# Token-shift mixes on GpSimd, a two-step first relu tile and a new written order in a fused attention and channel-mix kernel

## The chip, the cores and the metric

The kernel runs on one core of a Trainium2 chip. The metric is the device time of one execution in microseconds (us), and the median of several runs is compared. A separate profiled execution leaves the trace; its span runs from its first to its last instruction.

The engines are named as the profile names them: PE (TensorE matmuls; PEld its weight loads), DVE (VectorE), ACT (ScalarE), POOL (GpSimd) and SP (SyncE, which issues DMAs here). Each works through its own instructions strictly in the order given; semaphores make it wait for others.

## The reference

Eight batches, eight heads, 576 positions, head width 64. First an attention with exponential features, then a channel mix with a token shift:

```python
def phi(x):
    proj = np.einsum('bhsd,df->bhsf', x, w_phi)
    proj = proj - np.max(np.abs(proj), axis=-1, keepdims=True)
    return np.concatenate([np.exp(proj), np.exp(-proj)], axis=-1)
q_p, k_p = (phi(q), phi(k))
kv = np.einsum('bhsf,bhsd->bhfd', k_p, v)
z = np.sum(k_p, axis=2)
num = np.einsum('bhsf,bhfd->bhsd', q_p, kv)
den = np.einsum('bhsf,bhf->bhs', q_p, z)[..., None] + 1e-06
...
# x: the attention output, heads side by side, [8, 576, 512]
xk = mu_k * x + (1.0 - mu_k) * x_prev      # x_prev: x shifted by one position
xr = mu_r * x + (1.0 - mu_r) * x_prev
k = np.maximum(xk @ w_k, 0.0)              # 512 -> 1024
v = k * k @ w_v                            # 1024 -> 512
r = 1.0 / (1.0 + np.exp(-(xr @ w_r)))
return (r * v).astype(np.float32)
```

## The kernel before

**Tiles and stages.** Attention works on pairs of heads: 8 batches of 4 pairs, n = 0 to 31. The channel mix works on whole batches (the relu layer, gate and value layer on 512 positions each) and, for every two batches, on one edge tile that takes the remaining 64 positions of both.

**How the order is made.** Every piece of work is an `op` with a name, and the string `ORDER` (lines 19 to 129) lists all names in the order in which they are issued. A word is `name/ENGINE:place+n@i`: the engine, where the op allows several; the PSUM slot it is put into; and n filler matmuls (on a tile of ones) issued ahead of it. `Plan.op` (line 139) keeps the function, the engines allowed and the slots. Dependencies, costs and port marks in an op's arguments were meant for whoever writes the order; the program doesn't read them (the waits come from what the instructions read and write). So each engine's order is exactly the written one.

**The names.** A number after a name is the head pair n; `b.i` is a batch and a part.

- `lk`, `lq`, `lv`: loads of k, q and v for a batch or part of it, issued by POOL (v by POOL or SP). `wk`, `wr`, `wv`: weights, by POOL.
- `pt`, `pa`, `pb`, `tr`: transposes of q and k, on PE with copies for the first two batches, as DMA transposes issued by SP later (line 355).
- `kp`, `qp` (PE, line 570): projections of k and q. `rk`, `rq` (DVE, lines 583 and 588): their maxima of absolute values. `ea`, `eb` (ACT, line 609): the two exponentials of k. `mh`, `mt`, `mc`: q's maxima as two bf16 parts, transposed and copied, so that `qt` (PE, lines 634 and 640) can project q again transposed with the maximum subtracted; `qa`, `qb` (ACT, line 647) its exponentials. `tp`, `rt`, `mhe`, `mte`, `mce`, `ekt`, `qte`, `eqe` do the same for the edge positions of a whole batch; `em`, `eme` are exponentials of k's maxima.
- `va`, `vb` (line 601, POOL or DVE): v times those, the two right-hand sides of `kv` (PE, line 660). `kc` copies kv. `nd` (PE, line 681) is the numerator and denominator, `ra`, `rd` (DVE, lines 689 and 693) the quotient `x_sc`.
- `xt`, `xe`, `xf` (pairs 0 to 7: PE transpose and copies) or `xz`, `xu` (later pairs: DMA transpose issued by SP and a copy) put x into `xs`, features on partitions, shifted by one position. `df` (line 730, POOL or DVE) is `diff` = x - x_prev. `xa`, `xb` (line 736, DVE) are the two mixes, diff times mu plus x_prev, into `xk` and `xr`: one instruction each, 64 in all.
- `h` (PE, line 815): relu layer of a batch, eight tiles of 128 features, four matmuls each. `rl` and `sq` (lines 206 to 214): relu and square into `kk`. `r`, `th`: gate and tanh. `v` (PE, line 848), `ob` (DVE), `so` (SP): value layer, product, store. `he`, `rle`, `sqe`, `re`, `the`, `ve`, `obe`, `soe`: the same for the edge tiles.

**PSUM.** There are three slots P of two banks each and two slots M of one bank. The attention's projections, kv and nd take P; h takes M; r and v take M, in the last two batches P.

**Buffers around the change.** `diff` has two buffers, `xs` two, `vt` (v as loaded) three, q and k as loaded (`nat`) and transposed (`qkT`) two each, `kk` two. The first k and q arrive in float32 in a `kk` buffer (line 362). Three float32 tiles that are used at the start only, `wph_f32`, `ident_f32` and `sel3` (lines 223 to 228), have places of their own.

Of the kernel before, what the change touches and what calls it, by code (L numbers as in the profile page):

```python
# [19 lines left out]
ident ones hk hq dve2 hk.d hq.d wphi wphi.d lk0.1 lk0.1.d lq0.1 lq0.1.d mus mus.d lk0.2 lk0.2.d dve3  # L20
lq0.2 lq0.2.d lv0.0/POOL lv0.0.d lk0.0.d/ACT lq0.0.d/DVE pt0.0:0+9@0 pt0.1:1 pa0/ACT pb0/DVE tr0
dve1 tp0.0:0+1@2 kp0:1 rt0.0 qp0:2 rk0 ekt0.0 mhe0.0/POOL lk1.0 lk1.0.d mte0.0:0+4@1 rq0 pt1.0:0 ea0
pt1.1:1 lq1.0 lq1.0.d pa1/ACT mce0.0/DVE pb1/DVE tr1 lv0.1/POOL lv0.1.d eb0 tp0.1:0+1@4 qp1:2
lv0.2/POOL lv0.2.d rt0.1 rq1 eme0.0 kp1:1+1@1 mh0/POOL ekt0.1 qte0.0:0 mhe0.1/POOL em0 rk1 eme0.1
eqe0.0 lk1.2 lk1.2.d mte0.1:2+3@1 pt2.0:1 mce0.1/ACT mt0:0 pt2.1:0 mh1/POOL pa2/DVE ea1 pb2/DVE tr2
va0/POOL pt3.0:1+1@4 mc0/DVE qp2:2 em1 pa3/DVE mt1:0 eb1 pt3.1:0 mc1/DVE vb0/POOL rq2 qt0:0 kp2:1
qa0 lq1.2 lq1.2.d pb3/DVE tr3 kv0:2 rk2 qb0 lk2.0 lk2.0.d pt4.0:0 mh2/POOL kc0/DVE ea2 pa4/DVE
va1/POOL mt2:0+2@1 qp3:2 mc2/DVE eb2 qt1:0 rq3 wk.0 wk.0.d qte0.1:0 pt4.1:1 eqe0.1 tp0.2:1 vb1/POOL
qa1 rt0.2 pt5.0:0 nd0:2 pb4/DVE tr4 ekt0.2 mhe0.2/POOL pa5/DVE pt5.1:1 ra0 qb1 rd0 lv1.0/POOL
lv1.0.d kp3:1 rk3 wk.1 wk.1.d wk.d eme0.2 kv1:2+1@0 em2 qp4:0 wr.0 wr.0.d kc1/ACT rq4 pb5/ACT tr5  # L30
mte0.2:2+1@0 xt0:0 wr.1 wr.1.d wr.d ea3 pt6.0:1 vb2/POOL mce0.2/DVE pa6/DVE qp5:0 eb3 qt2:2 rq5
qte0.2:1 mh3/POOL qa2 kp4:1 va2/POOL xe0/DVE mt3:0 xf0/DVE em3 mc3/DVE rk4 pt6.1:0 qb2 mh4/POOL
kv2:0 df0/POOL eqe0.2 kc2/DVE nd1:2 pb6/DVE tr6 ea4 nd2:0 lq2.0 lq2.0.d ra1 rd1 pt7.0:0 eb4 va3/POOL
pt7.1:1 ra2 pa7/DVE qt3:2 pb7/ACT tr7 rd2 mt4:1 xt1:0 vb3/POOL qa3 xf1/DVE xe1/DVE tp1.0:0 mc4/DVE
qb3 rt1.0 wv.0 wv.0.d kv3:1 kc3/ACT kp5:2 xa0 ekt1.0 xt2:0 nd3:1 rk5 mhe1.0/POOL xf2/ACT eme1.0
xe2/ACT df1/POOL ra3 ea5 rd3 xb1 eb5 xt3:0+7@1 mte1.0:1 qt4:0 xa1 xf3/ACT xe3/ACT qp6:2 xb0
mce1.0/ACT qa4 qt5:1+1@1 df2/DVE tr2.0 tr2.0.d tr8 tr9 qte1.0:0 df3/DVE qb4 xa2 em4 xa3 qp7:0+3@1
qa5 vb4/POOL rq6 h0.0:1+1@1 qb5 lv1.2/SP lv1.2.d va4/POOL rq7 tr2.2 tr2.2.d tr10 tr11 kp6:2
rl0.0/ACT kp7:1 eqe1.0 vb5/POOL rk6 kv4:0 sq0.0/ACT h0.1:1 kc4/ACT mh6/POOL rk7 ea6 va5/POOL nd4:0
eb6 h0.2:0 ra4 lk3.0 lk3.0.d rd4 rl0.1/ACT kv5:2 lv2.0/SP lv2.0.d xb3 rl0.2/ACT mt6:0 h0.3:1 kc5/ACT  # L40
xb2 mc6/ACT em6 ea7 sq0.1/DVE qp8:0 vb6/POOL nd5:2 rq8 eb7 r0.0:0 va6/POOL ra5 rl0.3/ACT rd5 tp2.0:1
th0.0 qt6:0 sq0.2/POOL rt2.0 qp9:2 qa6 h0.4:0 lq3.0 lq3.0.d rq9 qb6 r0.1:1 sq0.3/POOL ekt2.0
rl0.4/DVE qp10:0 qt7:2 wv.1 wv.1.d wv.d rq10 th0.1 kp8:1 vb7/POOL qa7 h0.5:0 rk8 mhe2.0/POOL qb7
kv6:0 rl0.5/DVE xt4:1 sq0.4/POOL kc6/ACT kp9:2 ea8 nd6:0 rk9 va7/POOL h0.6:0 eb8 tr3.0 tr3.0.d tr12
# [116 lines left out]
def kernel(  # L161
# [120 lines left out]
    st = {}  # L282
# [516 lines left out]
    def add_moe(b):  # L799
# [240 lines left out]
```

## Time and profile before

| | us |
|---|---|
| three runs | 278.89, 276.7, 277.08 |
| median | 277.08 |
| the profiled execution, its own time | 277.05 |
| its span | 275.3 |
| granted TensorE clock, mean | 1.00 of full |

The chain of work that ended last, by engine and by line, is this:

```profile
PE 76%; ACT 9%; DVE 7%; issue 2%; DMA 2%; SPq 1%; POOL 1%; DVEq 0%; ACTq 0%; POOLq 0%
PE ps_v L848 19%; PE ps_h L815 17%; PE ps_r L834 10%; PE ps_nd L681 6%; PE ps_kv L660 5%; ACT q L647 4%; PE ps_qT L634 2%; PE ps_he L903 2%; PE ps_k L570 2%; ACT k L609 2%; PE ps_qT L640 2%; PE ps_q L570 2%; DMA vt<-in_v_dram 2%; PE ps_ve L935 2%; DVE nmk L583 2%
```

How the views are to be read: part 1 of the page has each engine's busy time (a union of its records), part 2 cuts the span into 40 equal slices and gives the busy share of each in tenths. A group of instructions has its line, engine, operation, what it writes and reads, shapes and count, then busy time and mean duration in ns, then the engine's idle time just before them and what ended most of it. A wait has who waited for whom, the total in us, how often, and the longest. The records of an engine overlap a little[...]; so where instructions follow closely, the step from start to start tells the cost better than the duration.

### The profile page before, as it was taken

The numbers are of one execution on the slowest core, as the hardware profiler recorded it, in microseconds if no ns is written. First come the engines' busy times: TensorE is split into PE (matmuls) and PEld (weight loads), VectorE is DVE, ScalarE is ACT, GpSimd is POOL, SyncE is SP. The second block draws the span as 40 slices with busy tenths as digits, with TensorE's granted clock in tenths as the row PEclk, the third lists the DMA queues.
The fourth block names the chain that finished last, engine by engine and source line by source line (L and its number), as shares of the span: only waits on it lengthen the run. The fifth ranks groups of instructions, "written<-read, shape, count | busy, mean of one in ns | idle before, by whom it ended". The sixth has DMA issues, their size and how long they took to land.

```text
span 275.3 us, 8896 instructions
## 1 busy us (share of the span) xinstructions
PE 260.7 (95%) x3692; PEld 153.8 (56%) x3736; DVE 229.5 (83%) x366; ACT 223.2 (81%) x410; POOL 157.8 (57%) x218
## 2 busy tenths in 40 slices
PE   7798999999999999999999899999999999999994
PEld 2465745565755655665565466565556654444552
DVE  5899999999999999999999799888849799834222
ACT  3699999999999999989989899999997855552430
POOL 5899827995858766596648863844565205111010
PEclk9999999999999999999999999999999999999999
DMA  7999999999997897979998899775244523504044
GB/s 152 217 234 231 205 189 196 204 147 241 203 185 139 200 219 165 206 209 182 197 187 166 130 194 208 176 229 64 64 116 100 63 62 66 133 5 116 2 114 114
DMA packets 65880, 42.89 MB, mean 156 GB/s; under 512 B 47152, under 2 KB 57008, under 8 KB 65840
## 3 DMA queue, kind: packets, MB, share of 16 engines
q1 hardware_dynamic: 54544, 27.77, 48.8%
q0 software_dynamic: 10992, 14.12, 29.6%
q8 instruction: 29, 0.48, 0.7%
q10 hardware_dynamic: 304, 0.43, 0.5%
q14 instruction: 11, 0.09, 0.1%
HBM read 33.62 MB, written 9.44 MB: 156 GB/s over the span
## 4 chain that ended last, share of the span: by engine, by line
PE 76%; ACT 9%; DVE 7%; issue 2%; DMA 2%; SPq 1%; POOL 1%; DVEq 0%; ACTq 0%; POOLq 0%
PE ps_v L848 19%; PE ps_h L815 17%; PE ps_r L834 10%; PE ps_nd L681 6%; PE ps_kv L660 5%; ACT q L647 4%; PE ps_qT L634 2%; PE ps_he L903 2%; PE ps_k L570 2%; ACT k L609 2%; PE ps_qT L640 2%; PE ps_q L570 2%; DMA vt<-in_v_dram 2%; PE ps_ve L935 2%; DVE nmk L583 2%
## 5 line engine op out<-in xcount | busy, mean ns | idle before, releaser
L601 POOL TENSOR_TENSOR v<-vt,v 128x576 bf16<-128x576 f32 x62 | 73.5, 1205 | 36.2 <-ACT v L595 33.5
L609 ACT ACTIVATE k<-ps_k 128x1024 bf16<-128x1024 f32 x64 | 64.0, 1042 | 1.3 <-DVE nmk L583 1.1
L647 ACT ACTIVATE q<-ps_qT 128x1024 bf16<-128x1024 f32 x64 | 63.0, 1042 | 2.2 <-PE ps_qT L640 2.0
L815 PE MATMUL ps_h<-xk,wk_bf 128*128 128x512 bf16 x239 | 62.3, 380 | 1.1 <-issue 0.2
L848 PE MATMUL ps_v<-wv_bf,kk 128*128 128x512 bf16 x240 | 58.2, 379 | 0.8 <-issue 0.2
L730 POOL TENSOR_TENSOR diff<-xs 128x576 bf16<-128x576 bf16 x21 | 28.1, 1347 | 30.9 <-DVE xr L736 19.1
L588 DVE TENSOR_REDUCE nmq<-ps_q 128x8 f32<-128x1024 f32 x32 | 38.7, 1216 | 1.1 <-PE ps_q L570 1.0
L848 PEld LDWEIGHTS <-kk 128*128 128x128 bf16 x256 | 23.8, 98 | 27.1 <-issue 0.2
L583 DVE TENSOR_REDUCE nmk<-ps_k 128x8 f32<-128x1024 f32 x32 | 38.5, 1217 | 0.5 <-PE ps_k L570 0.2
L854 DVE SCALAR_TENSOR_TENSOR ob<-rt,ps_v 128x512 f32<-128x512 bf16 x32 | 21.7, 684 | 18.0 <-PE ps_v L848 12.9
L815 PEld LDWEIGHTS <-wk_bf 128*128 128x128 bf16 x256 | 22.7, 98 | 24.7 <-issue 0.5
L206 ACT ACTIVATE krelu<-ps_h 128x512 bf16<-128x512 f32 x40 | 23.8, 607 | 15.2 <-PE ps_h L815 15.2
L834 PE MATMUL ps_r<-wr_bf,xr 128*128 128x512 bf16 x121 | 31.9, 380 | 0.4
L840 ACT ACTIVATE rt<-ps_r 128x512 bf16<-128x512 f32 x32 | 19.4, 608 | 14.7 <-PE ps_r L834 12.2
L214 POOL TENSOR_TENSOR kk<-krelu 128x512 bf16<-128x512 bf16 x17 | 17.8, 1047 | 18.2 <-ACT krelu L206 13.8
L693 DVE TENSOR_TENSOR x_sc<-ps_nd,rden 128x640 bf16<-128x640 f32 x32 | 26.0, 818 | 0.7
L736 DVE SCALAR_TENSOR_TENSOR xk<-diff,mu_k_t,xs 128x576 bf16<-128x576 bf16 x32 | 26.3, 836 | 0.1
L736 DVE SCALAR_TENSOR_TENSOR xr<-diff,mu_r_t,xs 128x576 bf16<-128x576 bf16 x32 | 26.3, 837 | 0.0
L660 PE MATMUL ps_kv<-v,k 64*128 64x65 bf16 x1024 | 22.7, 190 | 1.6 <-DVE x_sc L693 0.7
L208 DVE TENSOR_SCALAR krelu<-ps_h 128x512 bf16<-128x512 f32 x24 | 16.4, 683 | 8.8 <-PE ps_h L815 8.0
L660 PEld LDWEIGHTS <-k 64*128 64x128 bf16 x1024 | 19.7, 94 | 6.7 <-DVE nmq L588 1.5
L212 ACT ACTIVATE kk<-krelu 128x512 bf16<-128x512 bf16 x35 | 22.1, 641 | 1.3 <-DVE krelu L208 1.2
(105 smaller groups left out, 416.9 us busy)
## 6 DMA issues: line engine op xcount, KB each, us to landing
out_dram<-ob SPq DMA_DIRECT2D x70, 128.0 KB, 2.5
vt<-in_v_dram SPq DMA_DIRECT2D x12, 576.0 KB, 4.7
nat<-in_k_dram POOLq DMA_DIRECT2D x6, 576.0 KB, 6.8
nat<-in_q_dram POOLq DMA_DIRECT2D x6, 576.0 KB, 7.9
vt<-in_v_dram POOLq DMA_DIRECT2D x3, 576.0 KB, 6.7
wk_bf<-in_moe_w_k_dram POOLq DMA_DIRECT2D x2, 512.0 KB, 8.7
wv_bf<-in_moe_w_v_dram POOLq DMA_DIRECT2D x2, 512.0 KB, 8.5
nat<-in_k_dram POOLq DMA_DIRECT2D x3, 288.0 KB, 6.3
```

What stands on the lines that cost most here:

```text
L583: nc.vector.tensor_reduce(t[:, j, :], s["k"].rearrange("p a (g f) -> p (a g) f", f=128), axis=AX.X, op=ALU.max, apply_absolute_value=True, ...
L588: nc.vector.tensor_reduce(t[:, j, :], s["q"].rearrange("p a (g f) -> p (a g) f", f=128), axis=AX.X, op=ALU.max, apply_absolute_value=True, ...
L601: (nc.vector if eng == "DVE" else nc.gpsimd).tensor_tensor(vb[:, a, pn, :, 0:64], vt[b, a // 2][:, a % 2, :].rearrange("p (s d) -> p s d", ...
L609: nc.scalar.activation(s[f"k{pn}"], s["k"].rearrange("p a (g f) -> p (a g) f", f=128), AF.Exp, scale=(1.0 if pn == 0 else -1.0))
L647: nc.scalar.activation(t.rearrange("f x (a p) -> f x a p", a=2), s["qT"].rearrange("f a (x p) -> f x a p", p=64), AF.Exp, scale=(1.0 if pn ...
L660: nc.tensor.matmul(ps[:, hh, pn * 65:(pn + 1) * 65], lhsT=s[f"k{pn}"][r, c, :], rhs=vb[r, a, pn, 2 * g + par, :], start=(pn == 0 and c == ...
L693: nc.vector.tensor_tensor(s["x"].rearrange("p (b s) d -> p b s d", b=2), s["ndv"][:, :, :, 0:64], s["rd"].to_broadcast([128, 2, 5, 64]), o ...
L730: (nc.vector if eng == "DVE" else nc.gpsimd).tensor_tensor(s["d"], xs[:, a, 64:64 + S], xs[:, a, 0:S], op=ALU.subtract)
L736: nc.vector.scalar_tensor_tensor(out=t[:, a, (b % 2) * S:(b % 2 + 1) * S], in0=s["d"], scalar=mu[:, a:a + 1], in1=xs[:, a, 0:S], op0=ALU.m ...
L815: nc.tensor.matmul(ps, lhsT=wk_bf[:, c, fc * 128:(fc + 1) * 128], rhs=xkt[bp][:, c, m0:m0 + 512], start=(c == 0), stop=(c == NDC - 1))
L834: nc.tensor.matmul(ps, lhsT=xrt[bp][:, c, m0 + ci * 128:m0 + (ci + 1) * 128], rhs=wr_bf[:, c, :], start=(c == 0), stop=(c == NDC - 1))
L848: nc.tensor.matmul(ps, lhsT=s["kk"][:, fc, ci * 128:(ci + 1) * 128], rhs=wv_bf[:, fc, :], start=(fc == 0), stop=(fc == NFC - 1))
```

## The change

**Mixes.** `xa` and `xb` may now be placed on POOL. There a mix is two instructions: a product of `diff` and mu into a float32 tile `emix` (one buffer), and the sum of that and `xs`. The new order places 13 of the `xa` and 12 of the `xb` on POOL; 39 mixes stay on DVE as they were.

**First relu tiles.** Tiles 0 and 1 of the first batch, formerly `h0.0` and `h0.1` in two M slots, become one pair in a P slot, summed in two ops: `ha0` takes three of the four input chunks for both tiles (6 matmuls, needs `xa0` to `xa2`), `hb0` the fourth (2 matmuls, needs `xa3`).

**Constants.** `wph_f32`, `ident_f32` and `sel3` move into the `kk` buffer that already takes the first k and q.

**Dependencies given to the order's writer.** `ea` may stand ahead of `rk`, and `ekt` ahead of `rt`.

**Order.** `ORDER` is written anew from end to end. How often an op kind is on which engine, where this differs:

| op | before | after |
|---|---|---|
| xa, xb | DVE 64 | DVE 39, POOL 25 |
| df | DVE 11, POOL 21 | DVE 24, POOL 8 |
| va, vb | DVE 2, POOL 62 | DVE 11, POOL 53 |
| sq | DVE 12, ACT 35, POOL 17 | DVE 23, ACT 28, POOL 13 |
| sqe | DVE 1, ACT 4, POOL 3 | DVE 1, ACT 5, POOL 2 |
| rl, rle | DVE 25, ACT 47 | DVE 27, ACT 45 |
| kc | DVE 15, ACT 17 | DVE 12, ACT 20 |
| mc, mce | DVE 12, ACT 16 | DVE 19, ACT 9 |
| mhe | POOL 10 | DVE 5, POOL 5 |
| xe | DVE 5, ACT 3 | DVE 7, ACT 1 |
| xu | DVE 2, ACT 9, POOL 13 | DVE 1, ACT 12, POOL 11 |
| pa, pb | DVE 12, ACT 4 | DVE 13, ACT 3 |
| lv (issues) | POOL 5, SP 12 | POOL 3, SP 14 |
| filler matmuls | 36 | 30 |

The order around the first relu tiles, before and after (other stretches are rewritten in the same way):

```diff
-mce1.0/ACT qa4 qt5:1+1@1 df2/DVE tr2.0 tr2.0.d tr8 tr9 qte1.0:0 df3/DVE qb4 xa2 em4 xa3 qp7:0+3@1
-qa5 vb4/POOL rq6 h0.0:1+1@1 qb5 lv1.2/SP lv1.2.d va4/POOL rq7 tr2.2 tr2.2.d tr10 tr11 kp6:2
...
+xe1/DVE mhe1.0/DVE xf1/ACT kc3/ACT kp5:0 df1/DVE xf2/ACT ekt1.0 nd3:2 rk5 xb1/POOL eme1.0
+mte1.0:1+1@1 tr2.0 tr2.0.d tr8 tr9 ra3 ea5 mce1.0/DVE xe2/DVE qte1.0:1+1@1 rd3 qp6:1 xa1/POOL eqe1.0
+rq6 qt4:2+1@0 eb5 xt3:0 lv1.0/SP lv1.0.d qp7:1 xb0/DVE em4 qt5:0 xf3/ACT lv1.2/SP lv1.2.d qa4
+xe3/DVE df2/DVE lv2.0/SP lv2.0.d df3/DVE qb4 tr2.2 tr2.2.d tr10 tr11 xa2/DVE qa5 xa3/DVE ha0:2+7@1
+xb2/DVE qb5 hb0 xb3/DVE h0.2:0 rl0.1/ACT rq7 va4/POOL rl0.0/ACT qp8:0 rl0.2/ACT qp9:2 rq8 kp6:1
```

The code:

```diff
-    wph_f32 = consts.tile([128, F], FP, name="wph_f32")
+    kk0 = mm.tile([128, NFC, 512], BF, name="kk").rearrange("p a x -> p (a x)").bitcast(FP)
+    X2 = 2 * (S // 64) * D
+    wph_f32 = kk0[:, X2:X2 + F]
...
-    ident_f32 = consts.tile([128, 128], FP, name="ident_f32")
+    ident_f32 = kk0[:, X2 + F:X2 + F + 128]
...
         def mix(i):
-            def f():
+            def f(eng):
                 dct, mu = ((xkt, mu_k_t), (xrt, mu_r_t))[i]
                 t = dct[bp]
+                if eng == "POOL":
+                    e = mid.tile([128, S], FP, name="emix", bufs=1)
+                    nc.gpsimd.tensor_scalar(e, s["d"], mu[:, a:a + 1], None, op0=ALU.mult)
+                    nc.gpsimd.tensor_tensor(t[:, a, (b % 2) * S:(b % 2 + 1) * S], e, xs[:, a, 0:S], op=ALU.add)
+                    return
                 nc.vector.scalar_tensor_tensor(out=t[:, a, (b % 2) * S:(b % 2 + 1) * S], in0=s["d"],
                                                scalar=mu[:, a:a + 1], in1=xs[:, a, 0:S],
                                                op0=ALU.mult, op1=ALU.add)
...
+        def h2(c0, c1):
+            def f():
+                if c0 == 0:
+                    s["h2"] = ptile(("P", "hh"), "ps_hh")
+                else:
+                    s["kk"] = mm.tile([128, NFC, 512], BF, name="kk")
+                    for fc in range(2):
+                        s[fc] = s["h2"][:, fc, :]
+                        s["kr", fc] = mm.tile([128, 512], BF, name="krelu", bufs=BUFS["krelu"])
+                for fc in range(2):
+                    for c in range(c0, c1):
+                        nc.tensor.matmul(s["h2"][:, fc, :], lhsT=wk_bf[:, c, fc * 128:(fc + 1) * 128],
+                                         rhs=xkt[bp][:, c, m0:m0 + 512], start=(c == 0), stop=(c == NDC - 1))
+            return f
...
+            if b == 0 and fc < 2:
+                mo, hn = ("P", "hh"), "hb0"
+                if fc == 0:
+                    op("ha0", "PE", 1.3, ("un",) + t, h2(0, 3), mixa[0:3] + ["wk.d"], chain="h", alloc=[("P", mo)])
+                    op("hb0", "PE", 0.44, ("un",) + t, h2(3, 4), mixa + ["wk.d"], chain="h",
+                       alloc=[("krelu", ("krelu", f"{b}.{i}")) for i in range(2)] + [("kk", ("kk", b))])
```

## The prediction

> **What bounds the kernel now.** I read the page's parts 1, 2 and 5 first, then busy time in six stretches, then VectorE's order of time, then the waits. Part 1 and the 40 slices of part 2:
>
> ```profile
> PE 260.7 (95%) x3692; PEld 153.8 (56%) x3736; DVE 229.5 (83%) x366; ACT 223.2 (81%) x410; POOL 157.8 (57%) x218
> PE   7798999999999999999999899999999999999994
> DVE  5899999999999999999999799888849799834222
> ACT  3699999999999999989989899999997855552430
> POOL 5899827995858766596648863844565205111010
> ```
>
> TensorE looks busy from start to end, but its records overlap. In the last 40 us, where only 512-column matmuls run, one starts every 0.216 us. At such start-to-start steps all its needed work is 237.4 us: relu layer h 55.3, value layer v 55.3, gate r 27.6, their edge tiles 17.6, kv 18.2, nd 20.8, k and q projections 14.7, second projection 14.1, rest 13.8. The span is 275.3, so 38 us are lost. About 3.8 stand at the end (last product, last store). Placing the nd matmuls in the trace against the work ordered ahead of them gives the rest: 22.4 lost by 42.6 us, 25.2 by 60, 30.2 at nd19 (140.9 us), 34.1 at nd31 (228.4 us).
>
> What holds TensorE up? Busy time by stretch (us, then PE, PEld, DVE, ACT, POOL):
>
> ```profile
> 60.00:100.00 40.00, 39.28 (x669) 24.68 (x678) 38.57 (x60) 38.29 (x66) 29.99 (x42) 1.00 1.02 189
> 100.00:150.00 50.00, 49.37 (x766) 29.39 (x771) 48.21 (x67) 45.82 (x88) 33.15 (x39) 1.00 0.98 196
> 150.00:200.00 50.00, 48.80 (x738) 28.90 (x745) 43.30 (x65) 46.85 (x83) 29.24 (x40) 1.00 0.71 147
> 200.00:232.00 32.00, 31.63 (x431) 18.59 (x433) 25.74 (x46) 23.73 (x43) 11.94 (x18) 1.00 0.39 78
> ```
>
> VectorE is 96% busy to 150 us, 87% in the next 50. GpSimd always has room. VectorE's own steps, from its order of time (start, us, operation, count):
>
> ```profile
> 37.95 0.82 DVE L730 TENSOR_TENSOR diff<-xs 128x576 bf16<-128x576 bf16 x2
> 38.69 1.54 DVE L736 SCALAR_TENSOR_TENSOR xk<-diff,mu_k_t,xs 128x576 bf16<-128x576 bf16 x2
> 40.15 2.35 DVE L588 TENSOR_REDUCE nmq<-ps_q 128x8 f32<-128x1024 f32 x2
> ```
>
> Start to start, a difference takes 0.37, a mix 0.73, and a maximum (its next group starts at 42.41) 1.13. Now D is the VectorE work ordered up to the last result that a TensorE step needs, and P the TensorE work ordered ahead of that step. TensorE's loss there is at least D - P plus VectorE's idle time so far. At h0.0, D - P is 17.1 and the idle time 4.2; at nd19 it is 19.9 and 10.2, together 30.1 against the 30.2 found. So **VectorE is the wall up to about 141 us**; after that TensorE has a nearly full queue, and loses 3.9 more up to nd31.
>
> **What the Trainium skill says.** "SBUF — State Buffer", section "Who interferes with whom": VectorE with two SBUF inputs and a GpSimd instruction that reads SBUF exclude each other for a whole instruction. The trace agrees: one xk mix took 1.77 us instead of 0.81 because GpSimd had started 0.01 us earlier (one xr took 1.83 at 232 us); the other 62 mixes met nothing.
>
> ```profile
> 150.65 1.77 DVE L736 SCALAR_TENSOR_TENSOR xk<-diff,mu_k_t,xs 128x576 bf16<-128x576 bf16 x1
> 150.64 1.17 POOL L601 TENSOR_TENSOR v<-vt,v 128x576 bf16<-128x576 f32 x1 [0.86 <-ACT v L595]
> ```
>
> "GPSIMD Engine Reference", "Elementwise — side-by-side cycle accounting": about 2.6 cycles an element at 1.2 GHz for two inputs (estimate for 576: 1.25 us), about 1.8 at best for a tight one-input loop (0.86). The rows agree with the first: 1.2 and 1.35; no row shows the second.
>
> ```profile
> L601 POOL TENSOR_TENSOR v<-vt,v 128x576 bf16<-128x576 f32 x62 | 73.5, 1205 | 36.2 <-ACT v L595 33.5
> L730 POOL TENSOR_TENSOR diff<-xs 128x576 bf16<-128x576 bf16 x21 | 28.1, 1347 | 30.9 <-DVE xr L736 19.1
> L736 DVE SCALAR_TENSOR_TENSOR xk<-diff,mu_k_t,xs 128x576 bf16<-128x576 bf16 x32 | 26.3, 836 | 0.1
> ```
>
> **The change, part by part.**
>
> *Mixes.* 25 mixes leave VectorE: 25 x 0.73 = 18.3 us. On GpSimd the sum is a v-like operation, 1.12 from start to start. The product has no row: from below 0.67, by the slope between a 4-element cast (0.187) and a 63-element copy (0.237); from above 1.23, the step of a difference. I take 0.8. The sum waits for the product on its own engine, 0.08 as in the cast and subtract of mhl. One mix is then 2.0 us (1.85 to 2.45), 25 are 50. The single float32 buffer costs nothing more, its only user being GpSimd's ordered queue.
>
> *What comes back.* 13 differences (13 x 0.37 = 4.8), 9 v products (9 x 0.61 = 5.5), 11 squares (11 x 0.33 = 3.7), and smaller copies and casts, less three kv copies, about 3.2. VectorE's sum falls by only 1, 220.9 to 220.0. ScalarE loses 6 squares on balance, 2 x copies and some small ones, and gains 3 kv and 3 shift copies: 210.8 to 205.5. GpSimd gains 50 and loses 13 x 1.23 + 9 x 1.12 + about 9: 154 to 169, of 275. So **the totals decide nothing; the order does**.
>
> *Order.* The same reckoning with the new order, D - P at its worst steps: ha0 16.6 (h0.0 had 17.1), qte2.0 18.7 (19.3), qt12 20.4 (r1.0 had 19.8), qt18 19.1, v2.0 18.3, kv20 18.2 (nd19 had 19.9), v3.0 17.9, v4.0 16.7. With the idle times seen at equal D: 20.9 (before 21.3), 25.3 (25.9), 27.7 (26.9), 28.9 against 30.1 near P = 100 to 110. VectorE stays the wall longer, to v4.0 (D 180.3, about 195 us). There its idle time, growing at the 0.56 us in 10 that it showed from 35 to 142 us, would be 13.2, and TensorE's loss 29.9; before, it was 33 there. With 1.0 more to nd31 (as before from 195 us) and 3.8 at the end: 237.4 + 29.9 + 1.0 + 3.8 = 272.1, or 3.2 under the span. I keep half, 1.7: for 50 us more every VectorE wait counts in full, and new waits on GpSimd join.
>
> *GpSimd's queue.* xa0, xb1 and xa1 stand on it just ahead of the first relu step. df1 ends near 33.7, two mixes end near 37.7, and VectorE's xa2 near 39.7: cover 2 us, gone if a mix takes 2.45 and its queue is also 1 us late. Behind them wait va4 and vb4, which kv4 needs, and the queue's k and q loads. xa7 and xb7 stand ahead of h1.0 and r1.0, xb31 ahead of r7.0 with about 0.5 us to spare.
>
> *First relu tiles.* ha0 starts after three k mixes instead of four, hb0 adds the fourth quarter: the same 8 matmuls, so 0 us of work, at most 0.7 earlier (one mix). It holds a two-bank slot until both relus have read it; the projections have two others.
>
> *The rest.* Two loads of v move from GpSimd's to SP's queue behind the first DMA transpose (3.4 us of issue); their landing took 4.7 and va4 starts near 42.5, so they are covered if that transpose starts by 34, as the earlier q load allows (it waited for that load until 36.7). The constants moved into a kk buffer cost nothing: its next user comes after 80 us. k's exponential ahead of its maximum concerns the first two pairs; the maximum then waits for ScalarE. Six fewer filler matmuls (30 against 36) save nothing, being run in idle time.
>
> Sum: 275.3 - 1.7 = 273.6 of span. The run profiled took 277.05, 1.75 over its span, as good as the median 277.08. So **275.3**.
>
> **Rivals.** *Bigger gain*: the whole 3.2 comes, and spacing removes the 2 us that the two blocked mixes lost: span 270.5 to 272, time 273 (272.2 to 273.8). For it: D - P. Against it: the second block lay in the tail, off the wall.
>
> *No change*: GpSimd takes the place. The waits
>
> ```profile
> POOL v L601 <- ACT v L595: 33.5, 12, 7.3
> POOL diff L730 <- DVE xr L736: 19.1, 3, 12.7
> ```
>
> are room that does not lie where the mixes want it: before 34 us GpSimd idled only 4 us. If its queue makes kv4 to kv9 1.7 us late, the gain is gone: 277 (276 to 278).
>
> *Slower*: the port. GpSimd's long SBUF instructions grow from 103 (about 115 us) to 126 (134), the VectorE instructions with two SBUF inputs from 90 to 98. One that comes at random finds GpSimd running about 0.58 of the time to 230 us, and waits half of one, 0.55: 0.32 each. Of about 73 on the wall, a quarter losing their place would cost 5.8 us. Against it: 2 of 90 blocked now, so the written order holds on the chip. For it: no trace shows the product, and 0.45 more of it would shift all that stands behind it. Three blocks eat the gain, eight more make it 1% slower: 281 (279.9 to 284).
>
> That the change isn't made is out: the instruction lists show 25 products and 25 sums on GpSimd.
>
> **Numbers.** Likeliest, small gain: 0.50, own range 273.3 to 277.3. Bigger gain 0.14, no change 0.14, slower 0.22. About 1%, 2.8 us, is what these runs (276.7 to 278.9) can tell from no change: faster is under 274.3, slower over 279.9. A third of the first case and all but a little of the second are faster: 0.30. Within 1%: 0.46. Slower: 0.24, the slower case and a rest. The range from 271.8 to 281.5 takes in the bounds of the product (25 x 0.45 = 11 us on GpSimd, mostly in its idle time) and most of the slower case.
>
> **What would show it.** Right: the first ps_h starts near 39.8 instead of 40.7; nd19 near 139; VectorE busy over 92% from 150 to 195 us; the product 0.7 to 0.95 us; few VectorE mixes, squares or v products over 1 us. Wrong: the product near 1.2; many such stretched instructions, or GpSimd's idle time before v gone and kv held by v; VectorE under 95% busy before 150 us because of DMA or GpSimd.

## The result and the profile after

The changed kernel takes **302.24 us** (median of 4 executions, 301.33 to 305.41), the kernel before on the same chip 277.41 us: a ratio of 1.0908, with a 95% interval of 1.0811 to 1.1005. It is slower. The forecast of 275.3 us missed by 27 us; its range ended at 281.5. The profiled execution took 301.34 us, with a span of 299.6 (before 275.3). Some executions of a kernel are disturbed and show a lower granted clock: here and below times, ratios and intervals are those of the undisturbed ones, the median of all executions stands in brackets where it differs, and a star marks a kernel whose trace is of a disturbed one. Ratios are of means, so they can differ a little from the quotient of the medians.

Parts 1 and 2 of the page of the changed kernel:

```profile
PE 266.1 (89%) x3679; PEld 154.5 (52%) x3726; DVE 246.0 (82%) x391; ACT 219.7 (73%) x401; POOL 199.5 (67%) x225
...
PE   7888867979998979987999899979988999989994
...
DVE  5999999999998899779998998788899894444512
...
POOL 8699894787799793999059639729964028946000
PEclk9999997999999999999999999979999999999998
```

VectorE's busy time was to fall by about 1 us and has grown from 229.5 to 246.0. GpSimd has 199.5 where the forecast's sum gave 169 (in steps). TensorE's granted clock dips in slices 7 and 27 (and in the last); before, no slice was below 9. Its mean is 0.985, 1.00 before. Over the 237.4 us of needed matmuls that would be 3.6 us (an estimate, which supposes that a matmul takes longer as the clock is lower; no run isolates it). The groups say which instructions grew, first the products in the page's part 5, then VectorE's mixes in the list of VectorE's groups (after the bar busy us and mean ns):

```profile
L743 POOL TENSOR_SCALAR emix<-diff,mu_k_t 128x576 f32<-128x576 bf16 x13 | 22.4, 1721 | 14.3 <-DMA out_dram<-ob 7.3
...
L743 POOL TENSOR_SCALAR emix<-diff,mu_r_t 128x576 f32<-128x576 bf16 x12 | 20.8, 1736 | 2.9 <-DVE diff L735 1.8
```

```profile
L746 DVE SCALAR_TENSOR_TENSOR xr<-diff,mu_r_t,xs 128x576 bf16<-128x576 bf16 x20 | 21.6, 1086 | 1.2 <-POOL diff L735 1.1
L746 DVE SCALAR_TENSOR_TENSOR xk<-diff,mu_k_t,xs 128x576 bf16<-128x576 bf16 x19 | 17.7, 947 | 2.0 <-POOL diff L735 2.0
```

Two things stand here. The product takes 1.72 us; the forecast took 0.8 and held 1.23 for the upper bound. And a mix on VectorE, 0.836 on the mean before, has a mean of 1.086 or 0.947. Its undisturbed duration is still 0.81: 10 of the 39 are longer than 1 us, up to 3.18. Over all VectorE instructions with two SBUF inputs (mixes, differences, value products, squares), the excess over the undisturbed durations of 0.81, 0.45, 0.75 and 0.42 us is 15.0 us in 19 instructions, against 2.0 in 2 before.

The chain of work that ended last has changed as well. It accounts for only a third of the span, so its shares are not to be compared one by one, but TensorE's 76% of before are 14%, and GpSimd's 1% are 11%, with the product first among GpSimd's lines:

```profile
PE 14%; POOL 11%; DVE 5%; issue 2%; ACT 1%; DVEq 0%; POOLq 0%; ACTq 0%
PE ps_v L873 5%; POOL emix L743 5%; PE ps_h L825 3%; PE ps_r L859 2%; POOL kk L217 2%; POOL xk L744 2%; DVE v L606 2%; POOL xr L744 1%; PE ps_he L936 1%; PE ps_nd L686 1%; DVE ob L879 1%; DVE kk L217 1%; PE ps_ve L968 1%; DVE xk L746 0%; DVE krelu L211 0%
```

Busy time by stretch (us, then PE, PEld, DVE, ACT, POOL, clock):

```profile
35.00:60.00 25.00, 19.91 (x277) 10.99 (x278) 24.69 (x30) 19.22 (x34) 18.21 (x18) 0.93 0.85 152
60.00:100.00 40.00, 36.43 (x649) 22.39 (x658) 37.98 (x63) 36.53 (x61) 33.11 (x42) 1.00 1.06 178
100.00:150.00 50.00, 44.06 (x703) 26.09 (x713) 44.96 (x67) 42.59 (x75) 36.23 (x40) 1.00 0.96 185
150.00:200.00 50.00, 45.90 (x698) 27.72 (x707) 45.90 (x70) 42.82 (x84) 33.27 (x35) 0.98 0.91 168
```

TensorE's busy time from 100 to 150 us was 49.37 and is 44.06. Up to 100 us VectorE is counted busy nearly all the time (24.69 of 25 us, 37.98 of 40), but stretched time counts as busy in that. From 100 us on no engine is full, which is what a chain that passes from engine to engine looks like.

The loss of TensorE, reckoned as in the prediction (time of a step less the work ordered ahead of it), in us; five of the kernels run later stand beside it:

| loss at | before | after | a_sum_only | a_sum_em4_lv | a_tt_product | a_dve_reduce | a_sum_em4_lv_reduce |
|---|---|---|---|---|---|---|---|
| kv4 | 22.4 | 27.7 | 26.1 | 21.5 | 27.1 | 24.4 | 20.9 |
| nd13 | 28.2 | 38.0 | 33.2 | 30.3 | 39.7 | 31.5 | 27.6 |
| nd21 | 31.7 | 45.2 | 37.9 | 35.3 | 44.2 | 36.7 | 31.1 |
| nd31 | 34.1 | 55.4 | 40.1 | 37.5 | 49.0 | 43.5 | 33.2 |

The loss is spread over the whole run. Its first step, 5.3 us up to kv4, can be read instruction by instruction. VectorE and then GpSimd of the changed kernel, in order of time (start, us, operation, count, idle time ahead):

```profile
37.49 1.21 DVE L746 SCALAR_TENSOR_TENSOR xr<-diff,mu_r_t,xs 128x576 bf16<-128x576 bf16 x1
38.62 0.45 DVE L205 COPY xs<-ps_x 128x576 bf16<-128x576 bf16 x1
39.11 1.91 DVE L735 TENSOR_TENSOR diff<-xs 128x576 bf16<-128x576 bf16 x2
40.94 3.35 DVE L746 SCALAR_TENSOR_TENSOR xk<-diff,mu_k_t,xs 128x576 bf16<-128x576 bf16 x2
44.22 3.91 DVE L746 SCALAR_TENSOR_TENSOR xr<-diff,mu_r_t,xs 128x576 bf16<-128x576 bf16 x2
```

```profile
37.35 1.72 POOL L743 TENSOR_SCALAR emix<-diff,mu_k_t 128x576 f32<-128x576 bf16 x1
39.16 1.54 POOL L744 TENSOR_TENSOR xk<-emix,xs 128x576 bf16<-128x576 f32 x1
40.81 2.88 POOL L606 TENSOR_TENSOR v<-vt,v 128x576 bf16<-128x576 f32 x2
43.63 0.82 POOL L329 DMA_DIRECT2D nat<-in_k_dram  x1
44.48 2.30 POOL L606 TENSOR_TENSOR v<-vt,v 128x576 bf16<-128x576 f32 x2
```

Two k mixes took 1.54 us before and take 3.35 here, two r mixes (at 46.01 us before) 1.53 and now 3.91, behind value products of GpSimd; the second difference, 1.54 instead of 0.45, is behind GpSimd's sum. TensorE waits for the third and the fourth k mix, 1.58 us inside `ha0` and 0.62 ahead of `hb0`. In the lines that follow, the third holds four matmuls that start 0.43 us apart in place of 0.22, and the last waits for VectorE's maximum, which stands behind the r mixes:

```profile
42.71 1.02 PE L840 MATMUL ps_hh<-xk,wk_bf 128*128 128x512 bf16 x4 [1.58 <-DVE xk L746]
44.35 0.64 PE L840 MATMUL ps_hh<-xk,wk_bf 128*128 128x512 bf16 x2 [0.62 <-DVE xk L746]
44.78 1.92 PE L825 MATMUL ps_h<-xk,wk_bf 128*128 128x512 bf16 x4
...
49.32 0.40 PE L575 MATMUL ps_k<-wph,qkT 64*128 64x128 bf16 x8 [1.66 <-DVE nmq L593]
```

The three waits and the slower matmuls add up to 4.7 us, against 5.3 for the step. The granted clock is lower in the stretch from 40 to 50 us (0.83; before it was 1.00):

```profile
40.00:50.00 10.00, 6.14 (x41) 2.56 (x39) 10.00 (x7) 5.36 (x9) 7.23 (x9) 0.83 1.10 154
```

Before the change GpSimd had no work while VectorE did its differences and five of the mixes (35.8 to 40.2 us). It sat waiting for ScalarE's exponentials `em4`:

```profile
34.02 1.27 POOL L730 TENSOR_TENSOR diff<-xs 128x576 bf16<-128x576 bf16 x1
40.19 3.42 POOL L601 TENSOR_TENSOR v<-vt,v 128x576 bf16<-128x576 f32 x3 [4.89 <-ACT v L595]
```

The new order has `em4` further ahead on ScalarE, so the value products are free earlier, and run into the mixes.

### The profile page after: what moved, and what is told of

The parts are those of the page before. It is cut to its first block, busy times and chain, and to the rows that moved or that the text cites. A ratio compares the mean times of both kernels' runs of the same rounds, so it can differ in the third digit from the quotient of the medians.

```text
span 299.6 us, 8907 instructions
## 1 busy us (share of the span) xinstructions
PE 266.1 (89%) x3679; PEld 154.5 (52%) x3726; DVE 246.0 (82%) x391; ACT 219.7 (73%) x401; POOL 199.5 (67%) x225
## 5 line engine op out<-in xcount | busy, mean ns | idle before, releaser
L606 POOL TENSOR_TENSOR v<-vt,v 128x576 bf16<-128x576 f32 x53 | 63.0, 1210 | 18.4 <-ACT v L600 15.4
L825 PE MATMUL ps_h<-xk,wk_bf 128*128 128x512 bf16 x230 | 60.4, 384 | 3.8 <-ACT krelu L209 1.4
L873 PEld LDWEIGHTS <-kk 128*128 128x128 bf16 x256 | 23.8, 98 | 27.1 <-issue 0.4
L865 ACT ACTIVATE rt<-ps_r 128x512 bf16<-128x512 f32 x32 | 19.1, 601 | 24.4 <-PE ps_r L859 24.4
L825 PEld LDWEIGHTS <-wk_bf 128*128 128x128 bf16 x248 | 22.2, 98 | 28.2 <-issue 5.1
L859 PE MATMUL ps_r<-wr_bf,xr 128*128 128x512 bf16 x118 | 33.8, 394 | 1.8 <-POOL xr L744 0.8
L743 POOL TENSOR_SCALAR emix<-diff,mu_k_t 128x576 f32<-128x576 bf16 x13 | 22.4, 1721 | 14.3 <-DMA out_dram<-ob 7.3
L209 ACT ACTIVATE krelu<-ps_h 128x512 bf16<-128x512 f32 x37 | 21.9, 603 | 12.7 <-PE ps_h L825 8.9
L698 DVE TENSOR_TENSOR x_sc<-ps_nd,rden 128x640 bf16<-128x640 f32 x32 | 26.1, 821 | 0.6
L665 PE MATMUL ps_kv<-v,k 64*128 64x65 bf16 x1024 | 21.8, 191 | 2.8 <-DVE v L606 0.9
L575 PEld LDWEIGHTS <-qkT 64*128 64x128 bf16 x512 | 17.5, 95 | 12.0 <-issue 9.0
L743 POOL TENSOR_SCALAR emix<-diff,mu_r_t 128x576 f32<-128x576 bf16 x12 | 20.8, 1736 | 2.9 <-DVE diff L735 1.8
L735 POOL TENSOR_TENSOR diff<-xs 128x576 bf16<-128x576 bf16 x8 | 10.8, 1351 | 17.7 <-DVE xk L746 11.6
L746 DVE SCALAR_TENSOR_TENSOR xr<-diff,mu_r_t,xs 128x576 bf16<-128x576 bf16 x20 | 21.6, 1086 | 1.2 <-POOL diff L735 1.1
## 6 DMA issues: line engine op xcount, KB each, us to landing
nat<-in_k_dram POOLq DMA_DIRECT2D x3, 288.0 KB, 7.9
nat<-in_q_dram POOLq DMA_DIRECT2D x3, 288.0 KB, 8.1
```

The source lines that it names most:

```text
L606: (nc.vector if eng == "DVE" else nc.gpsimd).tensor_tensor(vb[:, a, pn, :, 0:64], vt[b, a // 2][:, a % 2, :].rearrange("p (s d) -> p s d", ...
L665: nc.tensor.matmul(ps[:, hh, pn * 65:(pn + 1) * 65], lhsT=s[f"k{pn}"][r, c, :], rhs=vb[r, a, pn, 2 * g + par, :], start=(pn == 0 and c == ...
L698: nc.vector.tensor_tensor(s["x"].rearrange("p (b s) d -> p b s d", b=2), s["ndv"][:, :, :, 0:64], s["rd"].to_broadcast([128, 2, 5, 64]), o ...
L743: nc.gpsimd.tensor_scalar(e, s["d"], mu[:, a:a + 1], None, op0=ALU.mult)
L825: nc.tensor.matmul(ps, lhsT=wk_bf[:, c, fc * 128:(fc + 1) * 128], rhs=xkt[bp][:, c, m0:m0 + 512], start=(c == 0), stop=(c == NDC - 1))
L859: nc.tensor.matmul(ps, lhsT=xrt[bp][:, c, m0 + ci * 128:m0 + (ci + 1) * 128], rhs=wr_bf[:, c, :], start=(c == 0), stop=(c == NDC - 1))
```

## The experiments

Two causes were to be told apart: the **length** of the mix on GpSimd (its queue is late for what waits behind it), and the **port** that GpSimd and VectorE's two-input instructions exclude each other from. Behind them stand the places of single steps in the order. All times are medians; ratios compare with the kernel before on the same chip. The excess is read from one trace of each kernel.

| kernel | executions | us | ratio, 95% interval | excess in stretched VectorE instructions, us (number) |
|---|---|---|---|---|
| the changed kernel | 4 | 302.2 | 1.0908, 1.0811 to 1.1005 | 15.0 (19) |
| a_sum_only | 2 | 285.2 | 1.0267, 1.0142 to 1.0393 | 5.2 (6) |
| a_tt_product | 2 | 290.8 | 1.0470, 1.0279 to 1.0661 | 15.1 (17) |
| a_all_dve | 2 | 296.7 | 1.0682, 1.0608 to 1.0755 | 7.3 (8) |
| a_em4_late * | 3 of 4 | 300.3 (301.1) | 1.0806, 1.0717 to 1.0895 | 14.9 (18) |
| a_sum_em4 * | 3 of 4 | 282.5 (283.4) | 1.0160, 1.0070 to 1.0250 | 1.7 (3) |
| a_dve_reduce | 2 of 4 | 288.5 (290.7) | 1.0368, 1.0267 to 1.0469 | 6.1 (9) |
| b_pool25 | 4 | 312.8 | 1.1236, 1.1160 to 1.1313 | 13.0 (18) |
| a_sum_em4_lv | 4 | 281.2 | 1.0117, 1.0065 to 1.0169 | 2.5 (3) |
| a_act_em4_lv | 4 | 288.0 | 1.0360, 1.0301 to 1.0418 | 4.3 (8) |
| a_tt_em4_lv | 4 | 287.6 | 1.0363, 1.0319 to 1.0407 | 11.5 (16) |
| a_one_step | 4 | 304.5 | 1.0957, 1.0891 to 1.1023 | 15.4 (19) |
| a_sum_reduce | 9 of 20 | 278.9 (282.4) | 1.0021, 0.9993 to 1.0050 | 0.2 (1) |
| a_sum_em4_lv_reduce | 13 of 20 | 277.7 (278.8) | 0.9996, 0.9965 to 1.0026 | 0.7 (2) |

### What the product costs

`a_prices` does the product in four forms in turn; the third takes 0.5 in mu's place.

```diff
-nc.gpsimd.tensor_scalar(e, s["d"], mu[:, a:a + 1], None, op0=ALU.mult)
+kind 0: nc.gpsimd.tensor_scalar(e, ..., mu[:, a:a + 1], ...)   # float32, line 748
+kind 1: the same into a bfloat16 tile                          # line 751
+kind 2: nc.gpsimd.tensor_scalar(e, ..., 0.5, ...)              # line 753
+kind 3: nc.gpsimd.tensor_tensor(e, s["d"], mu[:, a:a + 1].to_broadcast([128, S]), op=ALU.mult)  # line 755
```

> The changed kernel with the 25 products in four forms in turn, to price them: float32 result with mu from memory (as it is, 1.72 us), bf16 result with mu from memory, float32 result with the constant 0.5 (leaves mu out of those mixes), and a two-input product with mu broadcast. If the float32 result costs the time, the bf16 form is under 1.2; if reading mu does, the constant form is under 1.2; if the one-input operation is slow as such, both stay near 1.7 and the two-input form near 1.25.

Its groups on GpSimd:

```profile
L753 POOL TENSOR_SCALAR emix<-diff 128x576 f32<-128x576 bf16 x6 | 9.9, 1650 | 1.0 <-ACT tk L507 0.8
L751 POOL TENSOR_SCALAR emix<-diff,mu_k_t 128x576 bf16<-128x576 bf16 x4 | 6.9, 1724 | 7.5 <-DVE diff L735 7.3
...
L748 POOL TENSOR_SCALAR emix<-diff,mu_r_t 128x576 f32<-128x576 bf16 x3 | 5.3, 1778 | 0.1
```

and the form with two inputs, with minimum, median and maximum in ns:

```profile
L755 POOL TENSOR_TENSOR emix<-diff,mu_r_t x4: 1137/1148/1148, 101.1 to 213.5; 128x576 f32<-128x576 bf16 x4
```

The kernel took 299.6 us in its one execution. The result's type makes no difference (1.724 against 1.72), the scalar from a tile 0.07 us. It is the one-input form itself that is slow here, as the third case of the expectation had it: with one input less it takes 1.72 us where the two-input product takes 1.15. "GPSIMD Engine Reference", section "Engine selection", of the Trainium skill says that one-input work is "roughly line-rate" on GpSimd, and the forecast, which put one input below two, agrees with that. For this form and size the measurement decides against it: 1.72 us is twice the 0.86 estimated for a one-input loop in the prediction.

### How much is the length

```diff
 a_sum_only
-nc.gpsimd.tensor_scalar(e, s["d"], mu[:, a:a + 1], None, op0=ALU.mult)
-nc.gpsimd.tensor_tensor(t[...], e, xs[:, a, 0:S], op=ALU.add)
+nc.gpsimd.tensor_tensor(t[...], s["d"], xs[:, a, 0:S], op=ALU.add)
 a_tt_product
-nc.gpsimd.tensor_scalar(e, s["d"], mu[:, a:a + 1], None, op0=ALU.mult)
+nc.gpsimd.tensor_tensor(e, s["d"], mu[:, a:a + 1].to_broadcast([128, S]), op=ALU.mult)
 a_all_dve
-xa0/POOL ... xb1/POOL ... xa1/POOL ...
+xa0/DVE ... xb1/DVE ... xa1/DVE ...
```

> The changed kernel with the product left out of the 25 mixes on GpSimd: each is the sum of diff and x_prev alone, one instruction (so those parts of xk and xr are not scaled by mu). Length theory (a mix on GpSimd takes 3.0 us instead of the 2.0 that the forecast used, and all the loss hangs on that): with 1.3 us in its place the time falls below the forecast's premise, to 273 to 279 us, and VectorE's stretched mixes nearly vanish. Order theory (the new order loses by its loads, slots and places whatever a mix costs): it stays above 292. Lock theory (the number of two-input meetings counts, not the length): about half of the loss stays, 285 to 291.

> The changed kernel with the product of the 25 mixes written as a two-input product of diff and mu broadcast along the row (same result). Length theory: if that product takes about 1.25 us like the other two-input forms, a mix is 2.5 us, and the time lies well between: 284 to 294 us. Order theory: no change beyond 2 us from 302. Lock theory: as many meetings, each as long as before for the sum and 0.5 shorter for the product: 296 to 301.

> The changed kernel with all 64 mixes on VectorE, every instruction at the same place in the order. VectorE gets 18.3 us of work back, about 14 of it ahead of v4.0, the last step where it was the wall. Length theory: no long GpSimd mixes, so the loss is only that extra work: 237.4 + 29.9 + 14 + 5 = 286 span, 284 to 291 us. Order theory: 302 plus most of the extra work, above 305. Lock theory: two-input instructions on VectorE grow from 98 to 123 but those of GpSimd fall from 126 to 76: 288 to 294.

With the sum alone the time falls by 17.1 us, to 285.2: inside the range of the lock theory (285 to 291) and above that of the length theory (273 to 279). The two-input product gives 290.8: inside the range of the length theory (284 to 294) and below that of the lock theory (296 to 301). Neither theory fits both. By the medians, 1.15 us more for each of 25 mixes cost 5.6 us, and the next 0.57 us (1.72 less 1.15) another 11.5. That looks like a price of length that is small while the mix fits in GpSimd's idle time and steep beyond, but it is not shown: the interval of the middle kernel is some 10 us wide, and the last step changes the form as well.

Two things speak against either cause alone. With the shortest mix 7.8 us over the kernel before remain (3.9 to 10.9 by the interval), which length doesn't explain. And `a_tt_product` has as much stretching as the changed kernel, 15.1 against 15.0 us, and is 11.5 us faster: the sum of the stretching is not the loss.

All mixes on VectorE in the new order came out at 296.7, above the ranges of the length and the lock theory (284 to 291, 288 to 294) and below that of the order theory (above 305), so all three expectations failed. 18.3 us of work (25 times 0.73) come back to VectorE, while the differences, value products and squares that it took over from GpSimd stay, and so do 7.3 us of stretching. Which of these the expectation had too small is not separated.

### Whether the first step is em4's place

```diff
-... qp7:1 xb0/DVE em4 qt5:0 xf3/ACT ... qa5 ... xb2/DVE qb5 hb0 xb3/DVE ...
+... qp7:1 xb0/DVE qt5:0 xf3/ACT ... qa5 ... xb2/DVE qb5 em4 hb0 xb3/DVE ...
```

> The changed kernel with one step moved: the exponentials em4, which free the value products va4, vb4, va5 and vb5 on GpSimd, stand behind qb5 on ScalarE instead of ahead of qa4, so that these four products can only start when VectorE's six mixes and two differences of 38 to 46 us are nearly over. Theory C (the first loss, about 5 us of TensorE time up to the key-value product kv4, is a collision of the value products with that cluster; the rest is the length of the mix on GpSimd): the TensorE loss at kv4 falls from 27.7 to about 22.5 us, the cluster's mixes go back to 0.81 us each, and the time falls from 302 to 296 to 299 us. Theory D (the first loss is made by the relu tiles in two steps, or by the three early mixes on GpSimd): 300 to 304 us, loss at kv4 27 or more.

> The same move of em4 in the kernel whose mixes on GpSimd are the sum alone (the product with mu is left out there). If the length of the mix and the collision at 38 to 46 us are the two causes and add up (theory C): 285.2 less 4 to 6, so 279 to 281.5 us, within 1.5% of the kernel before. If the first loss has another cause (theory D): 284 to 286.5 us. If both causes are gone and the changed order were worth what was forecast for it: 274 to 277 us.

In the changed kernel the move brought 1.9 us by the medians, 3 expected at least, and the loss at kv4 fell to 25.9 in place of 22.5: a miss. The cluster of mixes is late there to start with, because the sum on GpSimd (39.15 us) meets the two differences, so `em4` is again not late enough; two r mixes still took 3.36 us. With the short mix the move brought 2.7 us of the 4 to 6 expected. The intervals overlap in both pairs, so neither gain is shown by the times alone. The trace shows that the local effect is real. Here is the later kernel `a_sum_em4_lv`, which has the same move, VectorE and then GpSimd:

```profile
38.23 0.81 DVE L735 TENSOR_TENSOR diff<-xs 128x576 bf16<-128x576 bf16 x2
38.97 1.54 DVE L744 SCALAR_TENSOR_TENSOR xk<-diff,mu_k_t,xs 128x576 bf16<-128x576 bf16 x2
40.42 1.54 DVE L744 SCALAR_TENSOR_TENSOR xr<-diff,mu_r_t,xs 128x576 bf16<-128x576 bf16 x2
```

```profile
34.87 1.28 POOL L742 TENSOR_TENSOR xk<-diff,xs 128x576 bf16<-128x576 bf16 x1
41.71 2.40 POOL L606 TENSOR_TENSOR v<-vt,v 128x576 bf16<-128x576 f32 x2 [5.57 <-ACT v L600]
```

GpSimd's idle time of before is back, the mixes have their 0.77 us again, the clock from 40 to 50 us is 1.00, and the loss at kv4 falls from 26.1 to 21.5 us, below that of the kernel before. Of these 4.6 us, 2.6 are left at nd31 (40.1 against 37.5), the second move told of below among them. So beside the short mix the first step is the collision, as theory C had it, but what reaches nd31 is about half of what it costs on the spot.

### The port by itself

```diff
-nc.vector.scalar_tensor_tensor(out=t[...], in0=s["d"], scalar=mu[:, a:a + 1], in1=xs[:, a, 0:S], ...)
+nc.vector.tensor_reduce(t[...], xs[:, a, 0:S].unsqueeze(2), axis=AX.X, op=ALU.max)
```

> The changed kernel with its 39 mixes on VectorE made a one-input maximum over single elements of xs (the mix is left out of these; GpSimd's 25 stay as they are). VectorE then needs the shared port only for its few differences and value products, so that GpSimd's products and sums can not stretch its mixes. Theory L (the port: about 13 us of stretched VectorE work are most of the loss): 285 to 292 us. Theory Q (GpSimd's queue is simply late by 25 times 1 us, and the stretching is a side show): 297 to 302 us. The one-input form may be 0.1 to 0.2 us shorter than the mix's 0.81 us, which by itself takes 4 to 8 us off VectorE's work, of which some 2 to 4 us could reach the end under either theory.

```profile
L746 DVE TENSOR_REDUCE xr<-xs x20: 735/743/747, 38.9 to 246.1; 128x576 bf16<-128x576 bf16 x20
L746 DVE TENSOR_REDUCE xk<-xs x19: 735/743/749, 42.1 to 233.5; 128x576 bf16<-128x576 bf16 x19
```

Among 39 of these, in the same places of the order and with the same GpSimd instructions, none is longer than 0.749 us, where 10 of 39 mixes were stretched. "SBUF — State Buffer", section "Who interferes with whom", says that on trn2 this operation never contends for the shared port, and the trace agrees. The time falls by 13.8 us. The edit takes away two things besides: the instruction is shorter (39 times 0.07, 2.7 us in all), and it doesn't read `diff`, so that VectorE no longer waits for GpSimd's differences (3.2 us of idle time ahead of the mixes in the changed kernel). If both reached the end in full, 7.9 us would be left for the stretching; if neither did, 13.8. Its excess fell by 8.9 (15.0 to 6.1). Theory Q, which called it a side show, is out.

Which GpSimd instructions stretch VectorE's? By what GpSimd ran at the time, the 15.0 us of the changed kernel fall to value products (7.2), sums of the mixes (4.8), squares (2.6) and the product, which is the longest of them, 0.4. That one is the mix at 37.49 us above, which ended 0.37 us ahead of the product (37.35 and 1.72 us) and not behind it. Three squares of VectorE ran wholly inside a product and were not stretched; here is one of them, GpSimd and then VectorE:

```profile
103.11 1.72 POOL L743 TENSOR_SCALAR emix<-diff,mu_r_t 128x576 f32<-128x576 bf16 x1
```

```profile
103.97 0.42 DVE L217 TENSOR_TENSOR kk<-krelu 128x512 bf16<-128x512 bf16 x1
```

In all runs with this product, no VectorE instruction of two SBUF inputs that met one running had to wait for its end. So for this form the rule that the prediction quotes, exclusion for a whole instruction, is not what the traces show. Behind sums, value products and squares VectorE's stretched instruction did end after theirs, by 0.3 to 0.6 us. So the product's harm is its length, which makes late what stands behind it, and hardly the port that it holds itself.

Both causes taken away at once, and the same with the two moves in the order (the edits are those above, joined):

> Both causes taken away at once: GpSimd's mixes are the sum alone (product left out), and VectorE's 39 mixes are the one-input maximum (mix left out), 0.74 us each. With the changed kernel at 302.2, the short mix at 285.2 and the mixes without the port at 290.7 us this completes a square. If the port acts by itself and adds to the length: 285.2 less 8 to 11, so 274 to 277 us. If the port does its harm mainly because the long mix sits on it, so that the short mix takes most of it along: 280 to 284 us, of which 39 times 0.07 us is VectorE's shorter work.

> As a_sum_em4_lv (281.2 us), with VectorE's 39 mixes as the one-input maximum. There about 4 us over the kernel before were left, with some 3 us of stretched mixes still among them. If these are what is left: 276 to 278.5 us. If the rest is the changed order itself (loads and GpSimd's queue, kv16 and the tail): 279.5 to 281.5 us.

The square, in medians: 302.2 with both, 285.2 without the length, 288.5 without the port, 278.9 without either, between the two ranges that were expected. The port, with what else that edit takes away, is worth 13.8 us beside the long mix and 6.3 beside the short one, or 5.4% and 2.5% by the ratios. The difference, 2.9 points, has an uncertainty of about 1.9 (the four intervals taken as independent). So **the two causes are not a sum**: with either taken away, less is left of the other. A late GpSimd queue meets VectorE's instructions where it did not before, which would tie the two together; that is argued and not separated by a run. With the two moves, 277.7 us (275.8 to 279.6) lies inside the first range expected, and the ratio of 0.9996 is no difference from the kernel before. What was left of `a_sum_em4_lv`, 3.5 us by the medians, thus goes with this edit: with the remaining 2.5 us of stretching, the shorter instruction or the wait for differences. With its mixes off VectorE the new order has no other cost that these runs can show, though one of the size of the 2.7 us of shorter instructions could hide behind them. Nor has it the gain that was forecast for it.

### The order against the placement

```diff
 b_pool25: the kernel before, mix(eng) and the place of the constants as in the changed kernel
-xa0 ... xb1 ... xa1 ...
+xa0/POOL ... xb1/POOL ... xa1/POOL ...
 a_one_step
-for fc in range(2):
-    for c in range(c0, c1):
+for fc in range(2 if c0 else 0):
+    for c in range(NDC):
```

> The kernel before in its own order, with the same 25 mixes done on GpSimd as product and sum at the places in the order where they stood for VectorE; nothing else of the change. If the costs are those of the mix on GpSimd (3.0 us against 0.81 us, port and queue), the order does not rescue it: 290 to 305 us. If the changed order is what loses the time: 278 to 284 us. If the changed order is itself a help against the long mix: above 305 us.

> The changed kernel with its first relu-layer tiles summed in one step, as before the change, at the same place in the order. If the two steps are a small help, as forecast (below 1 us): 302 to 304 us. If they are a part of the loss at 40 to 48 us: 297 to 300 us.

The same 25 mixes on GpSimd in the old order give 312.8 us, 10.6 more than in the new one, and the intervals stand apart. So the new order is a help to this placement. (The expectation put this above 305.) A part of the 10.6 may go through the clock, whose mean is 0.961 here and 0.985 in the changed kernel. With `a_all_dve` this makes a second square: 277.4 with neither, 312.8 with the placement alone, 296.7 with the order alone, 302.2 with both. Each costs time by itself, the placement more; the new order, which gives VectorE other work, suits only a kernel whose mixes are off VectorE. The relu tiles in one step gave 304.5, where 297 to 300 was expected if the two steps were a part of the loss; its interval overlaps that of the changed kernel, so they are no part of it, and a help too small to be shown.

### A second move in the order, and the product in other forms

```diff
 a_sum_em4_lv, a_tt_em4_lv, a_act_em4_lv: em4 late, and
-... tr3.2 tr3.2.d tr14 tr15 ... lv2.2/SP lv2.2.d ...
+... lv2.2/SP lv2.2.d tr3.2 tr3.2.d tr14 tr15 ...
 a_act_em4_lv: the product on ScalarE
+nc.scalar.activation(e, s["d"], AF.Identity, scale=mu[:, a:a + 1])   # e in bfloat16, two buffers
```

> As a_sum_em4 (mix on GpSimd = the sum alone, the product left out; em4 late), and the load of v for the pairs 10 and 11 (lv2.2) stands on SP ahead of the transposes tr3.2 instead of behind them. In a_sum_em4 TensorE lost 4.6 us at 72 to 77 us waiting for a value product whose v was issued at 64.8 us, just behind two loads of k and q of GpSimd's queue, and landed at 73.4 us. Theory E (what is left of the loss is such places where the written order holds on each engine but loads, products and mixes meet in another order in time): loss at nd10 falls from 30.9 to 25 to 27 us, and the time from 283.4 to 277 to 280.5 us. Theory F (the stage is held by the transfers in all, so that an earlier v makes something else late): 282 to 285 us.

> The changed kernel, whole, with the product in the two-input form (1.15 us in place of 1.72), em4 late and lv2.2 ahead of tr3.2. a_tt_product alone gave 290.8 us. If the two moves are worth here what they are worth beside the short mix (theory E): 283 to 287 us. If the mix of 2.4 us keeps GpSimd late and on the port, so that the moves are eaten by later collisions, as em4 late was in the changed kernel (302.2 to 301.1): 288 to 291 us.

> The same kernel with the whole mix: the 25 products with mu are done by ScalarE (an activation with mu as its scale, result in bf16), at the place in the order where GpSimd's product stood, and GpSimd keeps the sum. ScalarE gets about 25 times 0.65 to 0.75 us, 16 to 19 us, on a busy share near 78%; GpSimd's mix is as long as in the kernel with the sum alone. Theory E with ScalarE off the path: 278 to 284 us. If ScalarE's exponentials are held up by products that wait for their difference: 286 to 294 us.

The earlier load of v took 1.3 us off by the medians (282.5 to 281.2), with overlapping intervals, and the time lies between the ranges of the theories E and F: undecided. On the spot it did nearly what theory E expected: the loss at nd10 is 27.7 (25 to 27 expected, 30.9 without it). The two-input product with both moves gives 287.6, between the two ranges expected; 290.8 without them has a wide interval, so the gain of 3.2 is not shown. ScalarE's products take longer than expected (0.79 against at most 0.75):

```profile
L743 ACT ACTIVATE emix<-diff,mu_k_t 128x576 bf16<-128x576 bf16 x13 | 10.2, 785 | 0.8 <-POOL diff L735 0.7
L743 ACT ACTIVATE emix<-diff,mu_r_t 128x576 bf16<-128x576 bf16 x12 | 9.5, 791 | 0.0
```

The time, 288.0, is 6.8 over the kernel with the sum alone and in the second range expected: 19.7 us of ScalarE work are not free. Whether the work itself costs this or the waits that it makes is not separated. Both this kernel and the one with the two-input product are 14 us better than the changed kernel, and 10 to 11 worse than the one before. No experiment pointed to a version that beats the kernel before, and none did.

## Why the prediction was wrong

**What bounds the kernel.** Right as to before, where VectorE's wall gave the loss at nd19 to 0.1 us. After the change this bound was not reckoned again: D takes VectorE's instructions at their undisturbed durations, which they no longer had.

**The mix on GpSimd, 2.0 us.** The first step that failed. The product took 1.72 us in place of 0.8, outside the bounds of 0.67 and 1.23. From start to start a mix was 3.18 us (34.17 to 37.35): 1.81 to the start of the sum, 0.88 forecast, and 1.37 for the sum, 1.12 forecast. The upper bound was that of a two-input operation, which supposes that one input does not cost more than two. No row of the trace before held such an operation, and the slope from copies of 4 and 63 elements was no evidence for 576. Between `a_sum_only` and `a_tt_product`, a mix of 2.0 us stands near 288.7 us (285.2, and of the 5.6 us that 1.15 us more cost the share of 0.72 us; an interpolation, not run, and as uncertain as the 290.8). So about half of the miss, 13.5 us, is this term.

**"So the written order holds on the chip."** The second. The other half, from 288.7 down to 275.3, is put here by subtraction: the sum at equal work kept every VectorE instruction at its old duration. `a_dve_reduce`, 13.8 us faster, agrees in size, though the two halves are not a sum and the lower clock is in them. The order holds the sequence on each engine. That no GpSimd instruction meets a two-input one on VectorE is nowhere enforced; before it came about through waits, such as GpSimd's 4.89 us for `em4`. This was the rival called slower, by the port: the mechanism was right for GpSimd's two-input instructions, its size was not. A quarter of 73 instructions, each with a chance of 0.58 to wait 0.55 us, are some 11 blocks and 5.8 us; measured over the whole run are 19 blocks of 0.79 us on the mean, 15.0 in all. And the products, which that count took in, hardly block: 0.4 of the 15.0. Its own remark, that 0.45 us more of the product would shift all that stands behind it, was a remark about half of what came, 0.92.

**GpSimd's queue.** The cover of 2 us for the three early mixes was gone as said: the last of them ended at 40.7 us in place of 37.7. What stood behind it was not late for kv4 alone, but met VectorE's mixes.

**VectorE's saving, "keep half".** It didn't come. Even with the mix cut to the sum, the two moves made and the port out of the way, the new order equals the old one (0.9996) and does not win 3.2 us.

**First relu tiles, constants, loads of v.** The first relu matmul started at 40.39 us (40.68 before, forecast 39.8). `a_one_step` bears out a small worth. The constants cannot be seen in the loss. The loads of v landed in 7.1 us on the median instead of 4.7 as assumed, and one of them held a value product for 2.8 us.

**Tell-tales.** nd19 at 155.0 us (forecast 139, 140.9 before), the product above 0.95, many stretched instructions: all as named for wrong. VectorE's share from 150 to 195 us rose from 87% (to 200 us) to 91% (40.93 of 45), close to the 92% named for right, and misled, since a stretched instruction counts as busy.

## What to carry to other kernels

Take an operation that no trace shows at the price of a probe, not of its neighbours: one instruction in a form with one more input was 0.57 us cheaper here. Work given to GpSimd was paid for twice here, in its own length, which delays what stands behind it, and in what its two-input instructions do to the two-input instructions of VectorE that it meets, and a written order keeps sequence, not distance in time. Before you move a step forward, ask which wait it ends, and whether that wait was what kept two users of the port apart.

## What the runs showed of the hardware

GpSimd's product of a 128x576 tile with a value for each partition takes 1.72 us, with a constant 1.65, and as a product of two tiles (one of them a broadcast) 1.15. A VectorE mix of 0.81 us took up to 3.18 us when two GpSimd value products (2.30 us) ran one after the other: that one waited for both. The mix at 40.94 us got in between two, took 1.72, and the second value product then took 1.68 instead of 1.17. GpSimd's product of one input, 1.72 us long, stretched a mix that started 0.14 us behind it by only 0.40, and squares that started 0.85 us or more behind it not at all. VectorE's one-input reduction on the same data was never stretched (0.749 us at most). TensorE's granted clock was 0.83 from 40 to 50 us, where its busy time was 6.14 of 10 us.
